# Projections of 64-row matmuls issued in two passes, and a layer-norm buffer pair reused as a fifth slot for down weights

## The chip, the cores and the metric

The kernel runs on one core of one Trainium2 chip. Its time is the device time in microseconds (us) of one launch, the median of three runs. A profile comes from one further execution, recorded by the hardware profiler.

## What is computed

Two layers, each an attention part A and a gated linear unit B, both added to their input. There are S = 2048 tokens, D = 576 features, H = 32 heads of 18, and F = 4608 hidden units. Both layers use the same weights.

```
x = x + A(layernorm(x));  x = x + B(layernorm(x))     # and the same again

A:  q, k, v = x @ wqkv, by heads
    phi(z)  = [softmax(z @ w_phi), softmax(-(z @ w_phi))]
    kv = sum_s phi(k)^T v;   z = sum_s phi(k)
    o  = phi(q) kv / (phi(q) z + 1e-6);   result o @ wo
B:  ((x @ w_gate) * (x @ w_up)) @ w_down
```

## The kernel before, in words

**Tiles.** Tokens come in 16 tiles of 128 and 8 blocks of 256. The gate and up weights stay in SBUF; the down weights do not fit and are streamed from HBM again for every block: 18 chunks of 288 KB per block and layer (`t_wd`, L1138), into a ring `wdr` of four slots. A slot is loaded again when the down matmuls of its chunk have read it.

**A planner sets the order.** Nothing in the kernel is issued by hand. Every piece of work is a generator (a thread) that yields requests: operations for an engine, a buffer from a pool, an event. `Sched.run` (L323) walks through all threads with a modelled clock per engine, picks the request with the lowest estimated start (minus a bias by priority, L430), and writes it to that engine's list. These lists, with the semaphore waits that the recorded reads and writes need, are the program. The planner's durations are constants in the code. So an edit of a priority or of an estimate changes the order on every engine.

**A block of B.** `t_bmain` (L1183) takes a lock on the PSUM banks and issues nine quads of 72 gate/up matmuls (`gu_quad`, L1149; matmuls on L1170). They are 64-row matmuls: 576 is four and a half times 128, and so the array runs as two halves of 64 rows side by side, one half for partitions 0 to 63 and one for 64 to 127. A quad is issued as four parts of 20, 20, 16 and 16 matmuls. In the first two parts each half writes banks of its own; in the last two it adds to the banks of the other half, and the first matmul there waits for the other half's last write (the `order` keys). Six of the eight PSUM banks serve the quads; once the quads hold all six, the lock is "open" (L1204), and threads that ask with a fourth argument of True may take the other two. ScalarE copies the gate result out (L1219), VectorE multiplies it with the up result into `hT` (L1221). Then `t_down` (L1228) runs 36 steps of two 512-column matmuls (L1243) and two 64-column ones (L1246) in full 128-row mode, and `t_bepi` adds the result to x.

**Projections.** Q, K, V and the output projection of a tile are made by `proj` (L864). It offers two forms and the planner takes the one that fits the mode TensorE is in: ten full matmuls (L870), or 18 row matmuls (L878) in which each half first makes five matmuls for a bank of its own and then four for the other's:

```
for i, h in enumerate((u, 1 - u)):
    for k in ((0, 1, 2, 3, 4) if i == 0 else (0, 1, 2, 3)):
...
            order=[("row", banks[h], 1 - u)] if i == 1 and k == 0 else []))
...
row = [o for pr in zip(half(0), half(1)) for o in pr]
return ("pe2", full, row)
```

All 18 are one request, so they stand together in TensorE's list. The first matmul of the second pass (number 11 of 18) waits for the first pass by a semaphore that TensorE itself raises; the planner's model prices that wait at `SEM_LAT`, 64 ns.

**What surrounds it.** `t_aout` makes phi(q) with `softmax_front` (L887), multiplies by kv (L1082), projects with wo and adds to x (L1130). `t_ain` makes phi(k), `t_v` makes v, `t_kv` (L1006) sums kv for layer 2. While block b of layer 1 runs its gate/up stage, the output projections and Q of the next block, and then K and V of the finished block for layer 2, go between its quads. Tiles from number 4 on project Q and the output only "in row", that is while a lock is open or the block is held up (`in_row`, L619). `softmax_front` needs one of two `psb` buffers and one of four `sm` buffers. The block after next waits for this kv sum (L1396).

**Layer norms.** `t_ln` (L805) takes one of two pairs of `xln` buffers, computes statistics on VectorE (L816, L821), three small ScalarE operations, the normalized tile on GpSimd or VectorE (L838), and transposes it by DMA on SP's queue (L856) or, with `fast`, on TensorE (L850).

**Queues.** All DMAs here are issued by SP, in the planner's order: down-weight loads (L1145), transposes of `xln` (L856), of phi(q) (eT, L1061) and of the attention output (oT, L1119), and the stores.

Of the kernel before, what the change touches and what calls it, by code (L numbers as in the profile page):

```python
# [14 lines left out]
SEM_LAT = 64.0  # L15


class Tracker:
# [45 lines left out]
    def ready_time(self, deps):  # L64
        t = 0.0
        for d in deps:
            f = self.fin.get(d, 0.0) + SEM_LAT
            if f > t:
                t = f
        return t  # L70
# [159 lines left out]
class _Thread:  # L230
    __slots__ = ("gen", "prio", "req", "name", "deps_cache", "est", "t_ready", "seq", "alt")
    _n = 0

    def __init__(self, gen, prio, name):
# [8 lines left out]
        self.t_ready = 0.0  # L243


class Sched:

    def __init__(self, tracker):
# [15 lines left out]
        self.open = False  # L264
        self.alt_cost = {"dve": 1.0, "pool": 1.0, "act": 1.0}
# [57 lines left out]
    def run(self):  # L323
        tr = self.tr
        while True:
            progressed = False
            again = True
            while again:
                again = False
                for th in list(self.threads):  # L330
                    while th.req is not None and th.req[0] not in ("ops", "alt", "pe2", "dma", "acq", "acqn"):
# [38 lines left out]
                        elif kind == "prio":  # L370
                            th.prio = r[1]
                            self._advance(th, None)
                        elif kind == "delay":
# [22 lines left out]
            for th in self.threads:  # L396
# [13 lines left out]
                elif r[0] == "pe2":  # L410
# [4 lines left out]
                    est = max(self.free_at["pe"], tr.ready_time(deps), th.t_ready)  # L415
                    th.alt = ("ops", "pe", ops)
                elif r[0] == "ops":
# [4 lines left out]
                    est = max(self.free_at[eng], tr.ready_time(deps), th.t_ready)  # L422
# [7 lines left out]
                key = (est - self.bias.get(int(th.prio), 0.0), -th.prio)  # L430
# [8 lines left out]
            if r[0] == "ops":  # L439
# [4 lines left out]
                for o in r[2]:  # L444
                    deps = tr.deps_for(eng, o.reads, o.writes, o.excl, True, o.order)
                    if not first:
                        t = max(t, tr.ready_time(deps))
# [24 lines left out]
            self._advance(th, None)  # L472
# [54 lines left out]
class K:  # L527
    def __init__(self, nc, A_x, A_wqkv, A_w_phi, A_wo, B_w_gate, B_w_up, B_w_down, out):
# [10 lines left out]
        self.urgent = 4  # L539
        self.prio0 = (4, 4)  # L540
# [9 lines left out]
    def alloc(self):  # L550
# [28 lines left out]
        self.xln = A("xln", [128, 2 * self.NXP, 640], BF16)  # L579
        self.st = A("st", [128, 2 * self.NXP, 12], F32)  # L580
# [31 lines left out]
        self.g_wd = [g("wd%d" % i) for i in range(self.NWD)]  # L612
# [192 lines left out]
    def t_ln(self, tiles, sig, fast=False):  # L805
        s = self
        x_sb, xln, st, mv, lnv, rstd, xT = s.x_sb, s.xln, s.st, s.mv, s.lnv, s.rstd, s.xT
        pair = yield ("acq", "xlnp")
        n = len(tiles)
        js = range(n)  # L810
        sl = [2 * pair, 2 * pair + 1]
# [8 lines left out]
        for j in js:  # L820
# [10 lines left out]
               reads=mvk + [("epst",)], writes=[("lnv", pair)]),  # L831
            Op(160, (lambda e: e.mul(nm[:, s0:s1], mean2, -1.0)),
               reads=mvk, writes=[("nmean", pair)]),
            Op(205, (lambda e: e.activation(rstd[:, s0:s1], lnv[:, s0:s1], ACTF.Exp, scale=-0.5)),  # L834
               reads=[("lnv", pair)], writes=[("rstd", pair)]),
        ])
        for j in js:
# [3 lines left out]
                reads=[("x", ss[j], 0), ("x", ss[j], 1), ("nmean", pair), ("rstd", pair)], writes=[("xln", sl[j])])])  # L841
                for eng, dur in (("pool", 800), ("dve", 340))[:1 + fast]])
        yield ("ops", "act", [Op(240, (lambda e: e.copy(xln[:, s0:s1, 576:640], xln[:, s0:s1, 512:576])),
                                 reads=[("xln", sl[j]) for j in js], writes=[("xlnt", pair)])])
# [208 lines left out]
    def t_aout(self, L, st_):  # L1053
# [80 lines left out]
        yield ("sig", ("x1", L, st_))  # L1134

    def t_wd(self, L):  # L1138
        s = self
        wdv = s.wd.rearrange("(f p) d -> p f d", p=128)  # L1140
# [323 lines left out]
```

## Time and profile before

| what | us |
|---|---|
| three runs | 1220.47, 1219.82, 1218.64 |
| median | 1219.82 |
| the profiled execution | 1216.11 |
| its span, first to last instruction | 1214.4 |
| mean granted TensorE clock in it | 0.978 of full |
| gate/up matmuls L1170, busy | 584.9 + 583.3 + 160.9 |
| down matmuls L1243 and L1246, busy | 292.7 and 222.0 |
| row projections L878, busy | 40.3 + 34.6 + 20.2 + 20.2 |

Busy times of matmuls that run side by side or overlap in the pipeline are each counted in full, so they sum to more than the span. A group's row gives the line, the engine, output<-inputs, the shape and the count, then busy time and the mean ns of one, then the idle time just before such instructions and what ended it. "PEld" is TensorE's weight load, "SPq" the DMA queue of SP. In the timeline each row is start, duration, engine, line, and in brackets the idle time before it with its releaser.

### The profile page before, as it was taken

How to read it: one execution, taken by the hardware profiler on the slowest of the kernel's cores; microseconds unless marked ns; L12 is line 12 of the kernel's file. 1: busy time of each engine (PE TensorE's matmuls, PEld its weight loads, DVE VectorE, ACT ScalarE, POOL GpSimd, SP SyncE). 2: the span in 40 equal slices, each digit the busy share in tenths (PEclk: the TensorE clock that was granted, in tenths of full speed). 3: DMA queues.
4: the chain of work that ended last, by engine and by line, in shares of the span. 5: the costliest groups of instructions: out<-in, count | busy, mean ns of one | idle time of the engine just before them, and what ended most of it. 6: DMA issues, size and time to landing. Idle time of an engine off the chain costs nothing.

```text
span 1214.4 us, 33952 instructions
## 1 busy us (share of the span) xinstructions
PE 1106.5 (91%) x15384; PEld 814.9 (67%) x15446; DVE 612.0 (50%) x1243; ACT 379.8 (31%) x917; POOL 264.6 (22%) x258
## 2 busy tenths in 40 slices
PE   5885999999999999999998589999999999999997
PEld 3663767768586776758585367685858585858584
DVE  7797554736464563635254566262526262524131
ACT  6774232514142341514042343040404040312120
POOL 5693121313122140412022222020202020200000
PEclk8897999999999999999999799999999999999999
DMA  7473145361614535170605111727272736363514
GB/s 174 113 290 92 32 112 118 53 178 33 187 34 132 88 80 140 33 193 19 176 13 149 47 26 42 193 33 197 32 197 23 185 44 173 49 155 72 156 32 147
DMA packets 183276, 128.84 MB, mean 106 GB/s; under 512 B 101595, under 2 KB 181979, under 8 KB 181979
## 3 DMA queue, kind: packets, MB, share of 16 engines
q1 hardware_dynamic: 183130, 126.66, 42.8%
q8 instruction: 121, 1.98, 0.7%
q14 instruction: 25, 0.20, 0.0%
HBM read 100.73 MB, written 2.36 MB: 85 GB/s over the span
## 4 chain that ended last, share of the span: by engine, by line
PE 71%; DMA 15%; DVE 7%; ACT 3%; POOL 1%; issue 1%; SPq 0%; DVEq 0%; POOLq 0%
PE ps L1170 45%; DMA wdr<-in_B_w_down_dram 15%; PE ps L1243 11%; PE ps L878 9%; DVE ss L935 2%; PE ps L870 2%; PE ps L1246 2%; PE ps L1082 1%; PE ps L982 1%; POOL dd L949 1%; DVE dd L920 1%; DVE mxmn L906 1%; DVE mxmn L901 1%; DVE hT L1221 1%; ACT dd L928 1%
## 5 line engine op out<-in xcount | busy, mean ns | idle before, releaser
L1170 PE MATMUL ps<-xT,Wg 64*128 64x256 bf16 x4608 | 584.9, 270 | 1.6 <-ACT xT L852 1.6
L1170 PE MATMUL ps<-xT,Wu 64*128 64x256 bf16 x4608 | 583.3, 270 | 1.5 <-DVE hT L1221 1.5
L1170 PEld LDWEIGHTS ps<-xT,Wg 64*128 64x128 bf16 x4608 | 432.2, 94 | 36.1 <-issue 3.3
L1170 PEld LDWEIGHTS ps<-xT,Wu 64*128 64x128 bf16 x4608 | 432.6, 94 | 29.8 <-DVE hT L1221 2.9
L1219 ACT CAST gsb<-ps 128x512 bf16<-128x512 f32 x288 | 167.7, 582 | 638.0 <-PE ps L1170 636.3
L1221 DVE TENSOR_TENSOR hT<-ps,gsb 128x512 bf16<-128x512 f32 x288 | 198.0, 690 | 262.8 <-ACT gsb L1219 262.7
L1243 PE MATMUL ps<-wdr,hT 128*128 128x512 bf16 x1090 | 292.7, 381 | 31.1 <-DMA wdr<-in_B_w_down_dram 29.4
L1243 PEld LDWEIGHTS ps<-wdr,hT 128*128 128x128 bf16 x1152 | 112.4, 98 | 183.1 <-DMA wdr<-in_B_w_down_dram 65.3
L1246 PE MATMUL ps<-wdr,hT 128*128 128x64 bf16 x1152 | 222.0, 193 | 4.6 <-DMA wdr<-in_B_w_down_dram 1.0
L949 POOL TENSOR_TENSOR dd<-dd,ss 128x576 bf16<-128x576 bf16 x124 | 142.7, 1172 | 210.8 <-ACT ss L943 210.7
L838 POOL TENSOR_SCALAR xln<-x_sb,nmean,rstd 128x576 bf16<-128x576 bf16 x58 | 47.0, 820 | 551.0 <-ACT rstd L834 551.0
L1170 PE MATMUL ps<-xT,Wr 64*128 64x256 bf16 x1152 | 160.9, 271 | 0.0
L1268 DVE TENSOR_TENSOR x_sb<-ps,x_sb 128x512 bf16<-128x512 f32 x32 | 21.9, 686 | 232.7 <-PE ps L1246 232.7
L1246 PEld LDWEIGHTS ps<-wdr,hT 128*128 128x128 bf16 x1152 | 113.0, 98 | 0.0
L935 DVE TENSOR_REDUCE ss<-dd 128x64 f32<-128x1152 bf16 x64 | 86.1, 1347 | 25.2 <-ACT dd L930 25.1
L911 POOL TENSOR_TENSOR dd<-psb,mxmn 128x576 bf16<-128x576 bf16 x62 | 72.0, 1163 | 86.4 <-DVE mxmn L901 86.4
L1170 PEld LDWEIGHTS ps<-xT,Wr 64*128 64x128 bf16 x1152 | 59.1, 95 | 7.2
L901 DVE TENSOR_REDUCE mxmn<-psb 128x32 f32<-128x576 bf16 x64 | 47.8, 746 | 23.5 <-ACT psb L898 22.9
L898 ACT CAST psb<-ps 128x288 bf16<-128x288 f32 x128 | 46.6, 400 | 30.1 <-PE ps L878 16.1
L928 ACT ACTIVATE dd<-dd 128x576 bf16<-128x576 bf16 x64 | 43.8, 684 | 38.3 <-DVE dd L920 38.1
L906 DVE TENSOR_REDUCE mxmn<-ps 128x16 f32<-128x288 f32 x128 | 51.9, 447 | 0.1
L920 DVE TENSOR_TENSOR dd<-ps,mxmn 128x288 bf16<-128x288 f32 x128 | 51.6, 445 | 0.0
(78 smaller groups left out, 777.1 us busy)
## 6 DMA issues: line engine op xcount, KB each, us to landing
wdr<-in_B_w_down_dram SPq DMA_DIRECT2D x288, 288.0 KB, 3.4
Wg<-in_B_w_gate_dram SPq DMA_DIRECT2D x4, 1152.0 KB, 13.1
Wu<-in_B_w_up_dram SPq DMA_DIRECT2D x4, 1152.0 KB, 15.3
x_sb<-in_A_x_dram SPq DMA_DIRECT2D x8, 288.0 KB, 3.3
out_dram<-x_sb SPq DMA_DIRECT2D x8, 288.0 KB, 3.6
Wraw<-in_A_wqkv_dram SPq DMA_DIRECT2D x8, 144.0 KB, 3.1
xT<-xln SPq DMA_TRANSPOSE x58, 2.7
Wv<-in_A_wqkv_dram SPq DMA_DIRECT2D x1, 576.0 KB, 4.3
```

What stands on the lines that cost most here:

```text
L878: out.append(Op(61, (lambda e, h=h, k=k, st=(i == 0 and k == 0), sp=(i == 1 and k == 3): e.matmul(s.ps[:, banks[h], 0:N], L[r, k, :], Wm[r ...
L901: ops = [Op(665, (lambda e: e.tensor_reduce(mxmn[:, pz, 0, :], p3, AX.X, ALU.max)), reads=[("psb", pz, 0), ("psb", pz, 1)], writes=[("mx", ...
L906: ops.append(Op(370, (lambda e, h=h, pv=pv: e.tensor_reduce(mxmn[:, pz, 1, 16 * h:16 * h + 16], pv, AX.X, ALU.min)), reads=[("pbd", bank)] ...
L911: yield ("alt", [(eng, [Op(dur, (lambda e: e.tensor_tensor(d1, p3, mxb, ALU.subtract)), reads=[("psb", pz, 0), ("psb", pz, 1), ("mx", pz)] ...
L920: ops.append(Op(370, (lambda e, d2h=d2h, pv=pv, mnbh=mnbh: e.tensor_tensor(d2h, pv, mnbh, ALU.subtract)), reads=[("pbd", bank), ("mn", pz, ...
L935: Op(1320, (lambda e: e.tensor_reduce(ss[:, sm, :].rearrange("p (b g) -> p b g", b=2), e4, AX.X, ALU.add)), reads=s.ddk(sm, 0) + s.ddk(sm, ...
L949: yield ("alt", [(eng, [Op(dur, (lambda e, ev=ev, rb=rb: e.tensor_tensor(ev, ev, rb, ALU.mult)), reads=s.ddk(sm, br) + [("ss", sm)], write ...
L1170: out.append(Op(54.3, (lambda e, bank=bank, cs=cs, lhsT=lhsT, rhs=rhs, st=st, sp=sp: e.matmul(ps[:, bank, cs], lhsT, rhs, start=st, stop=s ...
L1219: yield ("ops", "act", [Op(540, (lambda e, g=g, gb=gb: e.copy(gsb[:, g, :], ps[:, gb, :])), reads=[("gu", gb)], writes=[("gsb", g)], excl= ...
L1221: yield ("ops", "dve", [Op(625, (lambda e, g=g, ub=ub, p=p: e.tensor_tensor(hT[:, p, :], ps[:, ub, :], gsb[:, g, :], ALU.mult)), reads=[(" ...
L1243: ops.append(Op(d_pe(512), (lambda e, lhsT=lhsT, bank=bank, slot=slot, fi=fi, f=f: e.matmul(ps[:, bank, 0:512], lhsT, s.wdr[:, slot, fi, 0 ...
L1246: ops.append(Op(d_pe(64) + 3, (lambda e, lhsT=lhsT, sl=sl, slot=slot, fi=fi, f=f: e.matmul(ps[:, Z, 64 * sl:64 * sl + 64], lhsT, s.wdr[:, ...
```

## The change

A row projection becomes two requests, passes of 10 and 8 matmuls. Between them other threads' requests may be placed. For a wait of TensorE on itself the planner now assumes 450 ns (`PE_SELF`). While a lock is open, a projection's thread has a `boost`: its key is lowered by 500, or, if its estimated start is more than 100 ns past the time TensorE is free, raised by 1500. K and V of layer 2 for tiles 0 to 13 now also project only "in row".

After the last norm of the first attention, `t_grow` takes the second `xln` pair out of its pool, and `wdx`, a view of its bytes, joins the ring of down weights as slot 4. The dependencies of the norms are kept by slot instead of by pair, and the two single-tile norms at a layer's start or end share one pair.

The diff's core (repeated renamings of keys and passing of arguments left out):

```diff
+PE_SELF = 450.0
...
-    def ready_time(self, deps):
+    def ready_time(self, deps, eng=None):
...
         for d in deps:
-            f = self.fin.get(d, 0.0) + SEM_LAT
+            f = self.fin.get(d, 0.0) + (PE_SELF if eng == "pe" and d[0] == "pe" else SEM_LAT)
...
+                        elif kind == "boost":
+                            th.boost = r[1]
+                            self._advance(th, None)
...
-                    est = max(self.free_at["pe"], tr.ready_time(deps), th.t_ready)
-                    th.alt = ("ops", "pe", ops)
+                    est = max(self.free_at["pe"], tr.ready_time(deps, "pe"), th.t_ready)
+                    th.alt = ("ops", "pe", ops, self.pe_mode)
...
-                key = (est - self.bias.get(int(th.prio), 0.0), -th.prio)
+                late = th.boost and est > self.free_at["pe"] + 100.0
+                key = (est - self.bias.get(int(th.prio), 0.0) - (self.hold if late else th.boost), -th.prio)
...
-            self._advance(th, None)
+            self._advance(th, r[3] if th.req[0] == "pe2" else None)
...
+        self.wdx = AT("wdx", [128, CH, D], BF16, nc.lookup_mloc(self.xln).addr + 2560)
...
-    def t_ln(self, tiles, sig, fast=False):
+    def t_ln(self, tiles, sig, fast=False, slot=None):
...
-        pair = yield ("acq", "xlnp")
+        if slot is None:
+            pair = yield ("acq", "xlnp")
+            sl = [2 * pair, 2 * pair + 1]
+        else:
+            sl = [slot]
         n = len(tiles)
         js = range(n)
-        sl = [2 * pair, 2 * pair + 1]
+        key = lambda name: [(name, sl[j]) for j in js]
...
-               reads=mvk + [("epst",)], writes=[("lnv", pair)]),
+               reads=mvk + [("epst",)], writes=key("lnv")),
...
-                       [("xln", sl[j]), ("xlnt", pair)], [("xT", ss[j])], 128 * 640 * 2, False, True, 1250.0)
-        yield ("rel", "xlnp", pair)
+                       [("xln", sl[j]), ("xlnt", sl[j])], [("xT", ss[j])], 128 * 640 * 2, False, True, 1250.0)
+        if slot is None:
+            yield ("rel", "xlnp", pair)
...
         row = [o for pr in zip(half(0), half(1)) for o in pr]
-        return ("pe2", full, row)
+        if s.sc.open:
+            yield ("boost", s.rboost)
+        if (yield ("pe2", full, row[0:10])):
+            yield ("ops", "pe", row[10:])
+        yield ("boost", 0.0)
...
         s.vx_of[(L, st_)] = vxs
+        if L == 2 and st_ < NS - 2:
+            yield ("when", s.in_row)
         gots = yield ("acqn", ["pb"], 2, True)
         banks = [g_[1] for g_ in gots]
-        yield s.proj(st_, s.Wv, "Wv", banks)
+        yield from s.proj(st_, s.Wv, "Wv", banks)
...
-        sm = yield from s.softmax_front(st_, ps_, s.Wk, "Wk", 2 if st_ >= NS - 2 else 1 if L == 1 else 0)
+        sm = yield from s.softmax_front(st_, ps_, s.Wk, "Wk", 2 if st_ >= NS - 2 else 1 if L == 1 else 0, None, L == 2 and st_ < NS - 2)
...
+
+
+    def t_grow(self):
+        s = self
+        yield ("wait", ("xT", 1, NB - 1))
+        pool = s.sc.pools["xlnp"]
+        yield ("when", lambda: 1 in pool["free"])
+        pool["free"].remove(1)
+        yield ("rel", "wd", s.NWD, 0.0)
+
+    def wslot(self, slot):
+        return self.wdr[:, slot, :, :] if slot < self.NWD else self.wdx[:]
...
                 slot = yield ("acq", "wd")
                 s.wd_slot[(L, b, c)] = slot
-                yield ("dma", s.g_wd[slot], (lambda e, slot=slot, c=c: e.dma_start(s.wdr[:, slot, :, :], wdv[:, CH * c:CH * c + CH, :])),
-                       (), [("wdr", slot)], 128 * CH * D * 2, False, True)
+                yield ("dma", s.g_wd[slot], (lambda e, slot=slot, c=c: e.dma_start(s.wslot(slot), wdv[:, CH * c:CH * c + CH, :])),
+                       (), [("wdr", slot)] + ([("xln", 2), ("xln", 3), ("xlnt", 2), ("xlnt", 3)] if slot == s.NWD else []), 128 * CH * D * 2, False, True)
                 yield ("sig", ("wd", L, b, c))
...
                 ops.append(Op(d_pe(512), (lambda e, lhsT=lhsT, bank=bank, slot=slot, fi=fi, f=f: e.matmul(
-                    ps[:, bank, 0:512], lhsT, s.wdr[:, slot, fi, 0:512], start=(f == 0), stop=(f == NF - 1))),
...
         def pair_done(b):
             yield ("wait", ("x1", L, 2 * b))
             if b == 0:
-                yield ("go", s.t_ln([0], [("xTB1", L)], True), 11, "lnB%d_0a" % L)
+                pair = yield ("acq", "xlnp")
+                yield ("go", s.t_ln([0], [("xTB1", L)], True, 2 * pair), 11, "lnB%d_0a" % L)
                 yield ("wait", ("x1", L, 1))
-                yield ("go", s.t_ln([1], [("xTB2", L)], True), 11, "lnB%d_0b" % L)
+                yield ("go", s.t_ln([1], [("xTB2", L)], True, 2 * pair + 1), 11, "lnB%d_0b" % L)
                 yield ("wait", ("xTB1", L))
                 yield ("wait", ("xTB2", L))
+                yield ("rel", "xlnp", pair)
                 yield ("sig", ("xTB", L, 0))
                 return
...
         def k2():
             yield ("wait", ("x2t", L, 2 * b))
             if last:
+                pair = yield ("acq", "xlnp")
                 for j in range(2):
                     yield ("wait", ("x2t", L, 2 * b + j))
-                    yield ("go", s.t_ln([2 * b + j], [("xTk", j)], True), 11, "k2ln%d" % j)
+                    yield ("go", s.t_ln([2 * b + j], [("xTk", j)], True, 2 * pair + j), 11, "k2ln%d" % j)
                 for j in range(2):
                     yield ("wait", ("xTk", j))
+                    if j == 1:
+                        yield ("rel", "xlnp", pair)
                     yield ("go", s.t_ain(2, 2 * b + j), 11 + (2 - j) / 100.0, "ain2_%d" % (2 * b + j))
...
+        sc.launch(self.t_grow(), 9, "grow")
```

## The prediction, made before the changed kernel was run

> **What bounds the kernel now.** I read the page first (engines, then the chain that ended last), then the groups of instructions by line, the sources of the two suspect lines, and last the timeline of single blocks.
>
> ```profile
> span 1214.4 us, 33952 instructions
> PE 1106.5 (91%) x15384; PEld 814.9 (67%) x15446; DVE 612.0 (50%) x1243; ACT 379.8 (31%) x917; POOL 264.6 (22%) x258
> PE 71%; DMA 15%; DVE 7%; ACT 3%; POOL 1%; issue 1%; SPq 0%; DVEq 0%; POOLq 0%
> PE ps L1170 45%; DMA wdr<-in_B_w_down_dram 15%; PE ps L1243 11%; PE ps L878 9%; DVE ss L935 2%; PE ps L870 2%; PE ps L1246 2%; PE ps L1082 1%; PE ps L982 1%; POOL dd L949 1%; DVE dd L920 1%; DVE mxmn L906 1%; DVE mxmn L901 1%; DVE hT L1221 1%; ACT dd L928 1%
> ```
>
> TensorE is the bound, and beside it stand the down-weight loads (15% of the chain) and the 64-row projections (L878, 9%). From about 123 us the program is 16 GLU blocks: a gate/up stage of 648 matmuls (L1170), then a down stage of 72 matmul pairs (L1243 with 512 columns, L1246 with 64). The first 123 us and the layer change at 670 to 710 us are chains of other engines, which this change hardly touches.
>
> One projection between two gate/up quads, as the weight loads show it:
>
> ```profile
> 152.55 0.57 PEld L878 LDWEIGHTS ps<-Wq,xT 64*128 64x128 bf16 x10
> 153.52 0.36 PEld L878 LDWEIGHTS ps<-Wq,xT 64*128 64x128 bf16 x8 [0.40 <-PE ps L878]
> 153.91 0.09 PEld L1170 LDWEIGHTS ps<-xT,Wg 64*128 64x128 bf16 x1
> ```
>
> and who waited at that line in the whole run:
>
> ```profile
> its engine sat idle before it (us, times) until:
>   PE ps L878: 31.8, 80
> ```
>
> After ten loads TensorE stops 0.40 us for its own first pass: the second pass adds into the bank that the other 64 rows wrote. 80 times is every row projection there is (1440 matmuls of L878 / 18). Next the last down stage, which holds nothing but down matmuls: SP's issues, then the windows view (the middle of the stage, the whole stage, one gate/up stage of layer 1):
>
> ```profile
> 1190.02 14.81 SPq L1145 DMA_DIRECT2D wdr<-in_B_w_down_dram  x14
> core 0: us, PE busy (x) PEld busy (x) DVE busy (x) ACT busy (x) POOL busy (x), PEclk, DMA share, GB/s
> 1191.10:1207.10 16.00, 14.12 (x107) 6.61 (x108) 0.00 (x0) 0.00 (x0) 0.00 (x0) 1.00 0.87 256
> 1188.80:1209.60 20.80, 18.73 (x142) 8.98 (x144) 1.29 (x2) 0.58 (x1) 0.00 (x0) 1.00 0.68 199
> 190.50:237.30 46.80, 46.07 (x802) 38.12 (x801) 30.12 (x58) 20.19 (x49) 13.54 (x14) 1.00 0.37 51
> ```
>
> Four of the 18 chunks of a block are there when it starts, 14 are fetched inside it, each issued only when a slot is read out. The DMA engines are at 0.87, not at 1, while TensorE waits for them.
>
> **Change 1: the split projection.** Quads follow one another every 3.93 us without a projection (7.86 for two) and 5.30 with one (148.73 to 154.03), so a projection takes 1.37. Streaming, it would take 9 pairs: a gate/up pair of 256 columns comes every 0.109, so one of 288 every 0.1226, and nine 1.10. The stop therefore costs 0.27, not 0.40, since matmuls still run during part of it. All of it is on TensorE inside a saturated stage: 80 x 0.265 = 21.2 us. After the change the second pass is held back until its planned wait is over, and a gate/up part of 16 to 20 matmuls (0.87 to 1.09 us) goes between. That exceeds the 0.40 wait. Quads already do this: their third part waits on the first, 20 matmuls back, and the trace shows no gap (150.80 to 150.91). The waiting instruction would hold everything behind it on TensorE, but at most for the old 0.40. Passes and gate/up matmuls are all in 64-row mode, so no mode change is added; only a second pass that slips behind the end of the stage would add two, at 0.22 each (188.61 to 188.83 is one). I count nine in ten hidden: **-19 us** (bounds 0 and -21.2).
>
> **Change 2: the fifth slot.** A down pair comes every 0.245 us, so a stage needs 72 x 0.245 = 17.64, or 0.98 per chunk. What each stage takes beyond that and beyond the other matmuls in it (0.6 to 3.2 us) I took from the first and last weight load of each: 4.1, 2.4, 2.9, 2.1, 3.2, 3.5, 3.2, 4.4 in layer 1 and 3.4, 2.6, 3.1, 3.4, 3.1, 2.8, 2.5, 3.1 in layer 2, together 49.8 us. The waits view names 29.4 of it as TensorE waiting for the loads; the rest is refilling after each stop.
>
> How much does one more slot return? In the last stage the fifth chunk was used 4.1 after the start, and from then the interval is 294,912 B / 256 GB/s = 1.15 (1.11 by SP's issues: 14.44 / 13). Chunk 18 is then ready at 4.1 + 13 x 1.15 = 19.1 and needed at 17 x 0.98 = 16.7: 2.4 late, plus 0.7 of refilling, which is the 3.1 measured. With five slots one chunk more is there at the start: 4.1 + 12 x 1.15 = 17.9, late by 1.2, if the interval stays. But one more load is then in flight too. At a DMA share of 1 instead of 0.87 the interval would be 1.00, the last chunk ready at 16.1, nothing late. Halfway, at 1.07, it is 0.3 late. I take 0.6 per stage with refilling: 49.8 - 16 x 0.6 = **-40 us** (bounds: one interval per stage, 16 x 1.2 = -19, and -50).
>
> Here a rule weighs in. The Trainium skill (DMA: Bandwidth & Descriptors, Anatomy of one DMA), in its fit for the GpSimd path, makes a transfer a fixed 2.0 us plus its bytes at 436 GB/s: an estimate of 2.7 us for 288 KB, nearly all latency. By it a loop over five slots needs (0.98 + 2.7) / 5 = 0.74 per chunk, and every stop would vanish: -50. The page of this run has a median of 3.4 us to landing, on SP's queue, with the engines at 0.87, so loads queue behind each other. The row decides: -40, not -50.
>
> **Change 3: what pays for it.** The second layer-norm pair goes after the first layer's norms. Two norms per block remain: stats at 191.81 with transposes issued at 196.90, then stats at 206.15. With 2.5 us of issuing and 2.7 to landing a pair is held some 10 us, and the two begin 14 apart, so they don't meet; if they did, the later one waits up to 10 us, covered by the 47 us until the next block (259.57). Cost 0. At the start a fifth load joins four on SP (73.84, 13.17 us for all): 3.3 us more, then SP is idle until the eT transposes at 104.11. Cost 0 to 1. At a stage's end five loads instead of four stand ahead of the two oT transposes, about 1 us on data that is used 8 us after the stage ends (198.27, against 190.27). Cost 0. The other waits that the second pair's reuse adds are on transposes that landed long before.
>
> **Change 4: boost, and layer-2 K and V only inside gate/up stages.** Counts stay: K and V of tiles 0 to 13 are row projections already (252 / 18 = 14 each). They bunch earlier, where VectorE is busier, and each holds its two banks one part longer. The Trainium skill speaks against such a step (TensorEngine Tiling (Array Packing), PSUM Bottleneck): tiling speeds TensorE, not the emptying of PSUM, which can become the bound. If it did, the 19 us would not be seen. The row says 30.1 of 46.8 us busy on VectorE and 20.2 on ScalarE; in a stage 2.1 shorter that is 67% and 45%. Between 208 and 232 us VectorE is at 17.1 of 24. Only bunching can hurt: 0 to 1 us in seven stages, I take **+3 us**. The layer change may be planned differently, by 4 us either way; I take 0.
>
> **Sum.** -19 - 40 + 3 = -56. The profiled execution took 1216.1 (its span is 1214.4); the median of the runs stands 3.7 above that. So 1160 profiled and 1219.8 - 56 = 1164 as median.
>
> **Rivals.**
> - *The loads are at their limit* (0.14). The interval stays at 1.15 and the fifth slot gives only its head start. For: 0.87 of share, 1.00 at best against 0.98 needed. Against: the closed loop of issue after reading. Then 1219.8 - 19 - 19 + 3 = 1185.
> - *The projection's stop moves instead of going* (0.12): no gate/up part is ready between the passes, or gate/up waits for VectorE. For: two banks serve all projections. Against: L1170 waited 3.1 us for anyone in the whole run (1.6 at Wg, 1.5 at Wu, in the groups). Then 1219.8 - 40 = 1180.
> - *Slower: the second K tile misses its window* (0.08). Today it starts at 233.99, just after the stage's last gate/up matmul (233.97), and its key-value matmuls end at 247.68. Under the new condition a K that isn't admitted before the stage ends waits until the next block stands still for it, since that block waits for this key-value sum: 13.7 us open in each of the stages 2 to 7, 82 in all, so 1164 + 82 = 1246; from five of six stages on the kernel is slower. It decides by the softmax buffer that K needs: the second Q gives it back at about 223, 11 us before the stage ends. Today one projection per quad is let in, which is what puts K so late; with the boost it goes at the next part. So I hold it unlikely.
>
> **How the numbers follow.** Main case 0.62, 1148 to 1178 (all 71 us returned gives 1149, the lower parts of both gains about 1178). Mixtures near no change 0.04, split evenly over the three signs. Within 0.2% (2.4 us) counts as no change, about what a measurement of this kernel can tell. Faster 0.89, same 0.02, slower 0.09. The range 1148 to 1190 takes in the first two rivals and leaves out the slow one.
>
> **What would show it.** Right: the line of the projections has no 0.40 stop in most of the 80, its 18 matmuls appear as 10 and 8 with gate/up between; gate/up stages with eight projections shrink from 46.2 to about 44; down stages from 20.7 to about 18.2 in the last block; the chain's share of down loads falls from 15% to a few per cent; DMA share in a down stage rises above 0.87. Wrong: SP's issues still 1.11 apart (first rival), L1170 waiting for VectorE (second), or gaps of over 10 us ahead of blocks 2 to 7 (third).

## The result, and the profile after

The changed kernel takes **1177.51 us** (median of four runs, 1173.66 to 1178.24); the kernel before took 1220.14 beside it (1218.64 to 1221.16). The ratio is 0.9645, 95% interval 0.9621 to 0.9669: 42.6 us less. The forecast was 1164, which is 56 us less. The profiled execution took 1178.24, its span is 1176.5 (1214.4 before), its mean granted TensorE clock 0.978, as before.

The page first: span, engines, and the two rows of the chain that ended last (gate/up is now L1203, down L1276 and L1279, the row projection L892, the full one L884).

```profile
span 1176.5 us, 34009 instructions
PE 1088.5 (93%) x15446; PEld 840.3 (71%) x15446; DVE 605.8 (51%) x1243; ACT 378.1 (32%) x917; POOL 264.5 (22%) x258
PE 74%; DMA 11%; DVE 8%; ACT 4%; POOL 1%; issue 1%; SPq 0%; DVEq 0%; POOLq 0%
PE ps L1203 41%; PE ps L1276 16%; PE ps L892 9%; DMA wdr<-in_B_w_down_dram 5%; DMA oT<-dd 4%; PE ps L884 2%; PE ps L1279 2%; DVE ss L953 2%; DMA wdx<-in_B_w_down_dram 1%; PE ps L1102 1%; PE ps L1002 1%; DVE mxmn L924 1%; DVE mxmn L919 1%; POOL dd L967 1%; DVE dd L938 1%; DVE hT L1254 1%
```

The down loads fell from 15% of the chain to 6 (5 for the ring of four, 1 for the fifth slot). But there is an entry that was not there before: `oT<-dd`, the transposes of the attention output, 4%. It makes up with them the 11% that DMA still holds.

The waits view of TensorE says the same (waited for: us in total, times, longest). Before:

```profile
PE ps L1243 <- DMA wdr<-in_B_w_down_dram: 29.4, 52, 1.6
```

and after:

```profile
PE ps L1276 <- DMA wdr<-in_B_w_down_dram: 11.3, 15, 1.8
...
PE ps L892 <- DMA oT<-dd: 7.8, 8, 1.6
...
PE ps L1276 <- DMA wdx<-in_B_w_down_dram: 1.6, 3, 1.1
```

29.4 us in 52 waits for down loads became 12.9 in 18, the fifth slot's included. And the source view of the row projections, where before stood one line, "PE ps L878: 31.8, 80":

```profile
its engine sat idle before it (us, times) until:
  DMA oT<-dd: 17.8, 16
  DVE x_sb L1150: 2.5, 14
...
```

TensorE's stop for itself is gone, in all 80 projections. A new wait is in its place, for data that was never waited for before. The view adds TensorE's two rows, matmuls and weight loads, so the 17.8 is not a time lost; the matmuls' own part is the 7.8 above.

The last down stage has no attention in it, in the forecast's trace and in this one. SP's issues:

```profile
1154.58 3.31 SPq L1178 DMA_DIRECT2D wdr<-in_B_w_down_dram  x4
1158.49 0.37 SPq L1178 DMA_DIRECT2D wdx<-in_B_w_down_dram  x1
1159.47 3.49 SPq L1178 DMA_DIRECT2D wdr<-in_B_w_down_dram  x4
1163.57 0.37 SPq L1178 DMA_DIRECT2D wdx<-in_B_w_down_dram  x1
1164.55 2.90 SPq L1178 DMA_DIRECT2D wdr<-in_B_w_down_dram  x3
```

and the windows view of its middle, of the same stretch of the stage before it, and of one gate/up stage of layer 1:

```profile
core 0: us, PE busy (x) PEld busy (x) DVE busy (x) ACT busy (x) POOL busy (x), PEclk, DMA share, GB/s
1155.50:1170.00 14.50, 14.14 (x115) 7.02 (x112) 0.00 (x0) 0.00 (x0) 0.00 (x0) 1.00 0.89 266
...
187.30:233.50 46.20, 45.05 (x794) 39.80 (x792) 30.93 (x61) 21.09 (x51) 14.66 (x14) 1.00 0.30 58
1102.00:1116.00 14.00, 13.99 (x115) 7.09 (x114) 0.00 (x0) 0.00 (x0) 0.00 (x0) 1.00 0.94 282
```

13 chunks are fetched inside the stage, not 14. They are (1164.55 + 2.90 - 0.37 - 1154.58) / 12 = 1.04 apart, where it was 1.11; in the stage before, the engines carry 0.94 and TensorE is busy 13.99 of 14.00. The last stage takes 18.22 (20.72 before; the forecast said about 18.2), the one before it 17.70 (20.15).

**Where the 37.9 us of span came from.** From the weight loads of each trace I cut the run into gate/up stages (first gate/up load to first down load), down stages (to the last down load), and the layer change. The sums of the 16 stages, in us, for all kernels that this text needs:

| kernel | first stage starts | gate/up stages | down stages | layer change | span |
|---|---|---|---|---|---|
| before | 123.00 | 693.2 | 350.7 | 39.36 | 1214.4 |
| after | 125.49 | 685.8 | 318.1 | 39.01 | 1176.5 |
| the split alone | 123.55 | 683.1 | 347.6 | 39.37 | 1201.7 |
| the fifth slot alone | 125.22 | 693.4 | 314.3 | 38.93 | 1180.0 |
| oT planned 3.2 us later | 125.74 | 684.8 | 312.4 | 40.48 | 1171.6 |
| oT planned 5.5 us later | 126.06 | 674.0 | 312.0 | 39.81 | 1160.0 |
| the same, 64 small matmuls ahead | 123.46 | 675.1 | 313.3 | 38.54 | 1158.6 |

Down stages gave 32.6 us (forecast 40), gate/up stages 7.4 (forecast 19 - 3 = 16), and 2.5 were lost ahead of the first stage. The large miss is in the gate/up stages: they lost their 80 stops and came out hardly shorter. A stage with eight projections took 47.0 us before in this cut and takes 45.5 to 46.7 now; the forecast had written 46.2 and 44.

**The new wait.** One gate/up stage of layer 2, starting at 811.54. SP's queue around its start, then the chain in the first microseconds:

```profile
807.73 3.31 SPq L1178 DMA_DIRECT2D wdr<-in_B_w_down_dram  x4
811.08 2.54 SPq L1139 DMA_TRANSPOSE oT<-dd  x2
```

```profile
811.08 6.16 DMA oT<-dd
817.24 0.05 issue
817.29 0.78 PE ps L892 x9
```

and the weight loads of the two projections that follow:

```profile
817.28 0.48 PEld L892 LDWEIGHTS ps<-Wo,oT 64*128 64x128 bf16 x10 [1.92 <-DMA oT<-dd]
...
818.90 0.45 PEld L892 LDWEIGHTS ps<-Wo,oT 64*128 64x128 bf16 x8
...
820.48 0.09 PEld L892 LDWEIGHTS ps<-Wo,oT 64*128 64x128 bf16 x1
820.73 0.48 PEld L892 LDWEIGHTS ps<-Wo,oT 64*128 64x128 bf16 x9 [0.16 <-DVE x_sb L1150]
```

The passes are 10 and 8, with gate/up matmuls between them (817.76 to 818.90): the split works as forecast. But the first output projection of the stage stands behind one quad of 72 matmuls, 3.9 us after the start, and its input lands 5.7 after it. Everything behind it in TensorE's list waits too. In the whole run eight gate/up stages have such a stop of the matmuls, two in layer 1 and six in layer 2.

### The profile page after: what moved, and what is told of

It reads as the page before. It is cut to its first block, busy times and chain, and to the rows that moved or that the text cites. A ratio compares the mean times of both kernels' runs of the same rounds, so it can differ in the third digit from the quotient of the medians.

```text
span 1176.5 us, 34009 instructions
## 1 busy us (share of the span) xinstructions
PE 1088.5 (93%) x15446; PEld 840.3 (71%) x15446; DVE 605.8 (51%) x1243; ACT 378.1 (32%) x917; POOL 264.5 (22%) x258
## 3 DMA queue, kind: packets, MB, share of 16 engines
q8 instruction: 121, 1.98, 0.7%
## 4 chain that ended last, share of the span: by engine, by line
PE 74%; DMA 11%; DVE 8%; ACT 4%; POOL 1%; issue 1%; SPq 0%; DVEq 0%; POOLq 0%
PE ps L1203 41%; PE ps L1276 16%; PE ps L892 9%; DMA wdr<-in_B_w_down_dram 5%; DMA oT<-dd 4%; PE ps L884 2%; PE ps L1279 2%; DVE ss L953 2%; DMA wdx<-in_B_w_down_dram 1%; PE ps L1102 1%; PE ps L1002 1%; DVE mxmn L924 1%; DVE mxmn L919 1%; POOL dd L967 1%; DVE dd L938 1%; DVE hT L1254 1%
## 5 line engine op out<-in xcount | busy, mean ns | idle before, releaser
L1203 PE MATMUL ps<-xT,Wu 64*128 64x256 bf16 x4608 | 589.7, 270 | 2.3 <-DVE hT L1254 1.9
L1203 PE MATMUL ps<-xT,Wg 64*128 64x256 bf16 x4608 | 585.1, 270 | 1.6 <-ACT xT L865 1.6
L1203 PEld LDWEIGHTS ps<-xT,Wu 64*128 64x128 bf16 x4608 | 432.1, 94 | 23.3 <-DVE hT L1254 5.3
L1203 PEld LDWEIGHTS ps<-xT,Wg 64*128 64x128 bf16 x4608 | 425.8, 94 | 28.8 <-issue 3.3
L1276 PE MATMUL ps<-wdr,hT 128*128 128x512 bf16 x924 | 241.8, 380 | 11.5 <-DMA wdr<-in_B_w_down_dram 11.3
L1203 PE MATMUL ps<-xT,Wr 64*128 64x256 bf16 x1152 | 202.4, 271 | 0.0
L1279 PE MATMUL ps<-wdr,hT 128*128 128x64 bf16 x924 | 178.1, 193 | 0.0
L1276 PEld LDWEIGHTS ps<-wdr,hT 128*128 128x128 bf16 x924 | 90.3, 98 | 121.3 <-DMA wdr<-in_B_w_down_dram 18.6
L1203 PEld LDWEIGHTS ps<-xT,Wr 64*128 64x128 bf16 x1152 | 92.1, 95 | 5.0
L1279 PEld LDWEIGHTS ps<-wdr,hT 128*128 128x128 bf16 x924 | 90.5, 98 | 0.0
L1276 PE MATMUL ps<-wdx,hT 128*128 128x512 bf16 x228 | 64.3, 380 | 1.9 <-DMA wdx<-in_B_w_down_dram 1.6
## 6 DMA issues: line engine op xcount, KB each, us to landing
Wg<-in_B_w_gate_dram SPq DMA_DIRECT2D x4, 1152.0 KB, 13.2
```

The costliest lines, as they stand in the source:

```text
L1203: out.append(Op(54.3, (lambda e, bank=bank, cs=cs, lhsT=lhsT, rhs=rhs, st=st, sp=sp: e.matmul(ps[:, bank, cs], lhsT, rhs, start=st, stop=s ...
L1276: ops.append(Op(d_pe(512), (lambda e, lhsT=lhsT, bank=bank, slot=slot, fi=fi, f=f: e.matmul(ps[:, bank, 0:512], lhsT, s.wslot(slot)[:, fi, ...
L1279: ops.append(Op(d_pe(64) + 3, (lambda e, lhsT=lhsT, sl=sl, slot=slot, fi=fi, f=f: e.matmul(ps[:, Z, 64 * sl:64 * sl + 64], lhsT, s.wslot(s ...
```

## The experiments

Ratios are against the kernel before on the same chip, with the 95% interval.

**1. The split alone** and **2. the fifth slot alone.** The first never launches the thread that hands over the second layer-norm pair; the second makes the projection one request again and takes out the boost, the planner's 450 ns and the condition on K and V (V's place is shown, K's is of the same kind):

```diff
-        sc.launch(self.t_grow(), 9, "grow")
```

```diff
-PE_SELF = 450.0
+PE_SELF = SEM_LAT
...
-        if s.sc.open:
-            yield ("boost", s.rboost)
-        if (yield ("pe2", full, row[0:10])):
-            yield ("ops", "pe", row[10:])
-        yield ("boost", 0.0)
+        yield ("pe2", full, row)
...
-        if L == 2 and st_ < NS - 2:
-            yield ("when", s.in_row)
...
```

> The changed kernel without its fifth slot: the second layer-norm pair stays in its pool, down weights keep four slots. First theory (the split's saving is mostly given back because the boost places the output projection before its transposed input has landed): down stages as before (20 to 23 us), gate/up stages as in the changed kernel, so only some 8 us are gained: 1212, between 1206 and 1216. Rival (the split saves its 19 us, and the two parts get in each other's way only together, a stage that ends sooner leaving less time for the transposes): 1201 or less.

> The changed kernel with its fifth slot, but each row projection again one request of 18 matmuls, no boost, no 450 ns in the plan, K and V of layer 2 not bound to the gate/up stages. Both theories give the fifth slot what the down stages lost between the two profiles, 33 us: 1187. If the parts help each other (a shorter gate/up stage matters to the loads) it is above 1192; if they hinder each other, below 1182.

Measured: split alone 1206.80, ratio 0.9918 (0.9892 to 0.9943), so 10.0 us; slot alone 1181.04, ratio 0.9708 (0.9676 to 0.9741), so 35.7 us. Their sum is 45.7, the whole change 42.6: within their intervals, some 3 to 4 us each, they add up, and no hindrance between the two is seen. The slot's part is near its 40. The split's part is half of its 19, and it is so without the slot: its gate/up stages sum to 683.1, 10.1 less than before. The split alone has the waits of the ring nearly as before, 25.6 us in 54 times; the slot alone 10.1 in 17. In the split alone the wait for the oT transposes is there as well, with four loads ahead instead of five, but smaller: 2.8 us on the matmuls, where the changed kernel has 7.8.

**3. The oT data planned later, by 3.2 us**, and **6. by 5.5 us**, from the time that the planner has SP's issue end (3200.0 in one, 5500.0 in the other; nothing waits on the chip, the planner only believes the data to come later and so orders the projection later):

```diff
+            if st_ >= s.urgent:
+                yield ("delay", s.sc.free_at["sp"] + 5500.0)
```

> The changed kernel, but the planner is told that the transposed input of an output projection (tiles from 4 on) is there 3.2 us after SP's issue ends. Nothing else differs on purpose. First theory: the waits of projection matmuls on the oT transposes (7.8 us on matmuls, 17.8 us on weight loads) go, and the gate/up stages of layer 2 shrink from 41.5 to 42.2 us to about 40.6: 1167 to 1171. Rival (the gate/up stages are long because of PSUM and VectorE, and the projection merely waits where it would wait anyway): no change, 1176 to 1179.

> The changed kernel, the planner told that the transposed input of an output projection is there 5.5 us after SP's issue ends, instead of 3.2 in the earlier try, which moved no projection past the landing (15.0 us of weight loads still waited for oT, against 17.8). Theory (the output projection is placed ahead of its data): the wait on oT goes to below 3 us and layer-2 gate/up stages come to about 40.6, in all 8 to 10 us: 1166 to 1170. Rival (the stages are long for another reason): the wait goes and the time stays at 1175 to 1178.

The smaller delay gave 1175.52, ratio 0.9665 (0.963 to 0.97), an expectation missed: it moved no projection past its landing, the weight loads still idle 15.0 us in 16 waits for oT, and the gate/up stages sum to 684.8. The larger one gave **1162.69** (1161.73 to 1164.11), ratio 0.957 (0.9551 to 0.9589), below the 1166 to 1170 expected. Its source view of the row projections has no line for oT any more:

```profile
its engine sat idle before it (us, times) until:
  DVE dd L938: 1.7, 10
  DVE x_sb L1152: 0.9, 3
  DMA xT<-xln: 0.2, 1
```

and the stage that answers to the one above starts at 804.23 with its first projection 6.9 us later, not 5.7:

```profile
811.12 0.57 PEld L892 LDWEIGHTS ps<-Wo,oT 64*128 64x128 bf16 x10
812.61 0.45 PEld L892 LDWEIGHTS ps<-Wo,oT 64*128 64x128 bf16 x8
```

No bracket: it waits for nothing. The transposes were issued at 803.76, as early as before relative to the stage. The gate/up stages sum to 674.0, so 11.8 less than in the changed kernel and 19.2 less than before, which is the forecast's -19. A layer-2 stage with four projections takes 41.04 (42.11 before, 41.53 to 42.98 in the changed kernel). This placement is what the split's gain had gone into: TensorE's stops on oT are 7.8 of the 11.8; the rest was not taken apart. The down stages are 6.1 us shorter as well, but that can't be put down to the placement: the smaller delay, which moved no projection past its data, has 312.4 there too, and TensorE's waits for down loads range from 7.5 to 14.2 us over kernels with the same ring (experiments 3 and 7).

**4. Without the boost**, and **5. without the boost and without K/V's condition** (taken out as in 2):

```diff
-        self.rboost = 500.0
+        self.rboost = 0.0
```

> The changed kernel with the boost at 0 (which also takes away the hold): passes still split, still priced at 450 ns, K and V still bound to the gate/up stages. First theory: projections go where they went before the change, so nothing waits for oT, and the split alone saves most of its 21 us: 1164 to 1170. Rival (without the boost K misses its window, or second passes follow the first without anything between): above 1180.

> The changed kernel with the boost at 0 and K and V of layer 2 no longer bound to the gate/up stages; passes stay split, the fifth slot stays. The run without boost alone left two gaps of 27 us ahead of blocks, where K had missed its stage, while its layer-2 gate/up stages were the shortest of all (39.18). If the missed K is all that was wrong there, this one keeps the 39.18 and has no gaps: about 1168, between 1162 and 1174. If the boost itself is needed (for the order on VectorE or for the banks), gaps remain and it is above 1180.

Without the boost: 1214.85, ratio 0.9984 (0.9963 to 1.0005): the whole gain is gone. TensorE's first waits are now

```profile
PE ps L1102 <- DMA eT<-dd: 42.5, 5, 14.2
PE ps L1276 <- DMA wdr<-in_B_w_down_dram: 11.6, 21, 2.0
```

and there are 27.83 and 27.28 us between a down stage and the next gate/up stage ahead of blocks 2 and 5, and 51.83 at the layer change. Each pass now takes a place of its own between two whole quads, as the chain shows (start, duration, what):

```profile
280.90 4.04 PE ps L1203 x72
284.94 0.61 PE ps L892 x10
285.55 3.93 PE ps L1203 x72
289.48 0.49 PE ps L892 x8
289.97 3.93 PE ps L1203 x72
```

With one pass per quad, eight projections need 16 places and a stage has nine. The second K and V come too late for the stage, their condition then lets them in only when a block is held up, and block 2 stands still until their kv sum is made: the slower rival of the forecast, in two of its six places (two more have 4.35 and 2.84 us) and at twice its 13.7 us, because the boost that it was said to depend on is gone. Output and Q projections run in the gap too, and the 13.8 us that TensorE waits there are for eT, which stands ahead of the kv sum in its list. The two passes together take 0.61 + 0.49 = 1.10, the forecast's streaming time.

With K/V's condition gone too: 1177.32, ratio 0.969 (0.9672 to 0.9707), the time of the changed kernel, and not the 1162 to 1174 expected. No gap is left between blocks, and no wait for oT, but the second K and V now run as full projections behind the gate/up matmuls. Gate/up and down stages together come to 650.9 + 341.2 = 992.1, 6.1 more than with oT planned later, and the layer change takes 49.91, 10.1 more: 16.2, and the spans are 15.9 apart (1175.9 and 1160.0). Why the layer change is longer I did not follow. So the boost is no luxury of the split: it keeps two passes inside one quad, and K and V inside the stage.

**7. The fifth slot handed over later**, at the end of the first block's attention instead of after the last norm, to see whether the slot costs the 2.5 us at the start:

```diff
-        yield ("wait", ("xT", 1, NB - 1))
+        yield ("wait", ("xTB", 1, 0))
```

> The changed kernel, the fifth slot joining the ring only when the norms of the first block of the first gated unit are done, not right after the attention's norms. If the first gate/up stage starts 2.5 us later than before the change because the planner sees a fifth load ahead of the eT transposes and reorders VectorE, it starts at about 123.3 again and the time falls by 2: 1175. If the late start has another cause it stays at 125.5 and 1177.

Measured 1177.80, ratio 0.9692 (0.9671 to 0.9713): no gain. The first stage starts at 123.90, but then takes 45.55 where it took 43.08; what was early was given back. The trace shows why: that stage now holds 36 of the matmuls that multiply phi(q) by kv (L1102), where the changed kernel's holds 24. The slot does reorder the start: it brings one eT transpose, and with it these 12 matmuls, ahead of the stage. The split alone, which has no slot, has 36 and 45.58. Counted to the end of the first gate/up stage, before stands at 167.3, the changed kernel at 168.6, the split alone at 169.1 and this one at 169.5; kernels with the slot and an unchanged order there reach from 166.5 to 169.1 (64 small matmuls ahead, oT 5.5 us later). So the 2.5 us at the start are in part work that changed places, and of the rest one profile of each kernel can't tell.

**8 to 10. What is left in the down stages.** 72 pairs of 0.245 make 17.64. In the changed kernel the last but one stage is at 17.70, others up to 21.38 (23.69 ahead of the layer change). The DMA table of the changed kernel's page has other queues than the data's (packets, MB, share of the 16 engines):

```profile
q1 hardware_dynamic: 183130, 126.66, 41.9%
q8 instruction: 121, 1.98, 0.7%
q14 instruction: 24, 0.20, 0.1%
```

On q8 there are 121 packets of 16 KB each, one for every 256 of TensorE's 30,892 matmuls and weight loads (30,892 / 121 = 255), and one lasts 0.88 to 1.86 us. The theory is that the DMA engine which carries it brings its part of a chunk later. In the changed kernel's trace (the stage ahead of the layer change left out, where attention runs) all seven stops of 0.5 us or more on a down load end 2.2 to 3.5 us after the start of such a packet. The last but one stage, whose packets come 0.6 us before its start and 17.3 us after it, has no stop. That is only a coincidence in time, so I moved the packets.

The first attempt added one-element memsets on engines that have nothing to do in the last two down stages, to have more instructions fetched (the spare tile and the later oT data are not shown):

```diff
+        if L == 2 and b >= NB - 2:
+            for eng, n, one in (("pool", 480, s.fill[0:1, 0:1]), ("dve", 220, s.fill[0:1, 1:2])):
+                yield ("ops", eng, [Op(60, (lambda e, one=one: e.memset(one, 1.0)), reads=[("hT", NP - 1)], writes=[("fill", eng)])
+                                    for _ in range(n)])
```

> This is the version with the later oT data (1162.69 us), and in each of the last two down stages GpSimd runs 480 and VectorE 220 one-element memsets into a spare tile from the moment that the stage begins; both engines have nothing else to do there. The memsets add nothing to what the stage's matmuls need; what they add is instructions to be fetched, some 1,400 of them. So far 14 of the 16 down stages hold an instruction packet of 16 KB (0.88 to 1.95 us on one DMA engine), most of their stops come 2.2 to 3.9 us after one, and the last but one stage, at 1082.70 to 1100.55 in that version, holds no packet in any trace and took 17.70 to 18.00 us. Theory: a packet of instructions holds up one sixteenth of a down load and that stops the matmuls, so the last but one stage now holds one to three packets, shows a stop of 0.3 to 1.8 us some 2 to 4 us after a packet, and takes 18.3 to 20 us; the last stage the same; 1164 to 1167 in all. Rival: the stops come from the loop of five slots and the packets only happen to fall there; packets appear, the last but one stage stays at 17.7 to 18.1 with no stop above 0.3, and the time stays within 1161 to 1164.

It took 1210.68, ratio 0.9952 (0.9935 to 0.9969), and tells little. The edit itself has a fault: the memsets count as readers of `hT`, so VectorE's next write there waited for all of GpSimd's, and the last gate/up stage took 68.64 us for 35.48. And the 1,400 added instructions came on q14, 35 packets there instead of 24, of 8 KB each; q8 still had its 121. The last but one stage took 18.19, with one stop of 0.31. Undecided.

The second attempt shifts TensorE's own packets. 64, or 32, one-column matmuls go ahead of the first transposes, where TensorE waits 5.3 us for its first data. All other instructions keep their order on every engine; each packet comes 128, or 64, instructions earlier in the program. Both are made from the version with oT 5.5 us later:

```diff
+            if which == "k" and kt == 0:
+                yield ("ops", "pe", [Op(0, (lambda e, bank=bank: e.matmul(s.ps[:, bank, 0:1], s.ident[:], s.ident[:, 0:1], start=True, stop=True)),
+                                        reads=[("ident",)], writes=[("pbd", bank)], excl=[("pb", bank)]) for _ in range(64)])
```

> The version with the later oT data (1162.69 us), with 64 one-column matmuls put ahead of the first transposes, where TensorE waits 5.30 us for its first data; nothing else differs in any engine's order. In that version a 16 KB instruction packet comes once in 256 instructions of TensorE (213 to 303 between two in the trace). 64 matmuls are 128 instructions with their weight loads, so each packet comes 128 instructions earlier in the program: some 8 us earlier in a down stage (288 instructions in 18 us). Theory: the packet causes the stops of the down stages, so they move with it. The last but one stage, which had no packet and no stop on a load, gets one about half way and a stop of 0.3 to 1.5 us 2 to 4 us behind it; stages 9 to 13, which had one 4 to 8 us after their start and stops of 0.25 to 0.9 us, lose it to the stage before or to its first us, where five slots are full, and lose these stops. Time 1159 to 1165. Rival: the loop of five slots causes the stops; they stay in the stages and at the chunks where they were (0.35, 0.76, 0.25, 0.89 us in stages 10 to 13, none in the last but one).

> As the one before with 32 matmuls, 64 instructions, some 4 us earlier in a down stage. Theory: the last but one stage gets a packet about 12 us after its start and a stop of 0.3 to 1.5 us behind it; the packets of stages 9 to 13 come 1 to 4 us after the start and their stops are gone or below 0.4 us; the last stage's packet comes about 8 us after its start with its stop behind it. Time 1159 to 1165. Rival: the stops stay where they were.

Times 1162.97 (ratio 0.9542, 0.951 to 0.9574) and 1162.77 (0.9534, 0.9501 to 0.9567): as without the shift. But the stops moved. When the stop ends and how long TensorE had waited, in three stages of layer 2, with the packet's start:

| stage | no shift | 64 matmuls | 32 matmuls |
|---|---|---|---|
| 11 | packet +6.7 us, stop +9.5 of 0.76 | packet +15.5, stop +18.3 of 0.52 | packet +1.9, no stop above 0.45 |
| 13 | packet +7.9, stop +10.6 of 0.89 | packets +0.7 and +16.7, no stop above 0.30 | packet +3.3, no stop above 0.46 |
| 14 | packets -0.6 and +16.5, no stop | packet +8.6, none above 0.25 | packet +13.2, stop +15.3 of 1.23 |

(times from the stage's start; stages counted from 0). The expectations of 8 and 9 say that stage 14, the last but one, holds no packet; the trace has one at each of its edges and none between. Stage 14 had stopped for at most 0.31 in the changed kernel and in every one made from it with the boost, five slots and the packets in place; with the shift of 32 it got its packet at 1099.77, and this is the weight loads' timeline behind it (the bracket is the weight loads' idle time, 1.53; the matmuls' own is 1.23):

```profile
1100.27 0.10 PEld L1284 LDWEIGHTS ps<-wdr,hT 128*128 128x128 bf16 x1
1101.90 0.10 PEld L1281 LDWEIGHTS ps<-wdr,hT 128*128 128x128 bf16 x1 [1.53 <-DMA wdr<-in_B_w_down_dram]
```

In both shifted kernels together 10 of 14 stops of 0.5 us or more end 2.1 to 3.4 us after a packet's start, though a stretch of 1.9 to 4.1 us behind the packets covers only some 2.2 of a stage's 19 us. Where the packet falls matters: in the changed kernel and the two shifted ones together, such a stop follows none of 16 packets in the first 4 us of a stage, 6 of 15 from 4 to 10 us, and 11 of 16 later (the stage ahead of the layer change and packets in a stage's last 2 us left out). As the stops moved with the packets and nothing else in the order changed, I take the packets for the cause of most long stops; that full slots absorb the early ones is my reading, not tested. Not all stops are theirs: four of the 14, 0.51 to 0.63 us, have no packet at that distance, and stage 14 took its packet at +8.6 without one. Moving the packets only moved the loss; I know of no edit here that avoids it.

## Why the prediction was right and wrong

**Direction, and what bounds the kernel: right.** TensorE with two kinds of stop; both were cut, and the time fell.

**Change 1, the projection's stop, -19: right in mechanism, and returned in full only with another placement.** No self-wait is left in 80 projections. The changed kernel kept 7.4 us of stage time and the split alone 10.1; with oT planned later it is 19.2. (For the price of a mode change the forecast points to 188.61 to 188.83; the place is 1188.61 to 1188.83, and the 0.22 stands.)

**Change 3, "Cost 0" for the oT transposes: the step that failed.** It said that five loads instead of four stand ahead of them, "about 1 us on data that is used 8 us after the stage ends". The 8 us were read from the trace of before, where the projection stood behind two quads (198.27, against 190.27). They were not a property of the data but of the order, and the same change moves the order: with the boost the projection goes at the first part after one quad, 3.9 us after the start. In the stage shown the data takes 6.16 us from issue and lands 5.7 us after the start. Over all 28 transposes that SP issues from oT's line, the time from issue to landing was, before and after:

```profile
DMA to landing us min/median/max: 2.6/4.1/5.5
DMA to landing us min/median/max: 2.6/4.7/6.2
```

The fifth load made them 0.6 to 0.7 later, so the "about 1 us" was right. But the new placement leaves some 0.5 before the stage's start and 3.9 after it, 4.4 in all, less than even the median. The split alone, with four loads ahead (2.6/4.2/5.5), waits too: the earlier use makes the wait, and the later landing lengthens it, from 2.8 to 7.8 us on the matmuls. How the 11.8 divide between the two is not settled: the split alone stands 9.1 above the 674.0, but 2.5 of that are its first stage with its 12 more matmuls.

The price is 685.8 - 674.0 = 11.8 us of gate/up time in the profiles. By time it is less sharp: the ratios 0.9645 and 0.957 are 0.0075 apart, 9 us, while experiments 7 and 6, timed on one chip (1177.80 and 1162.69), are 15.1 apart, 7.1 of it in down stages by their profiles.

**Change 2, the fifth slot, -40: right, a little high.** 32.6 us of stage time in the changed kernel, 36.4 in the slot alone, 38.7 with oT later; by times 35.7. The forecast left 0.6 us per stage; the changed kernel's down stages stand 32.6 below, so 7.4 / 16 = 0.46 more than that is left. The interval was taken at 1.07, measured 1.04 in the last stage. Most of the long stops that are left, which the sum did not have, follow instruction packets (experiments 9 and 10). The price that the fit of the Trainium skill (DMA: Bandwidth & Descriptors, Anatomy of one DMA) would give, every stop gone at -50, was not reached; chunks landed in a median of 3.6 us in the last stage, longer than the 3.4 of before and than the 2.7 that the forecast worked out from the fit. With one more in flight they queue a little more, as the forecast chose.

**Change 3 at the start, "Cost 0 to 1": not settled.** The first stage starts 2.5 us later in this profile, 0.5 to 3.1 with the slot in others; to the end of that stage it is 1.3, and part of the start is work that changed places (experiment 7).

**Change 4, +3 for VectorE: not seen.** With the boost in force, oT later and all 80 stops gone, the gate/up stages are at the full -19.2; VectorE has 30.93 of 46.20 us in the stage shown. What the boost costs is the early oT. What it saves is the whole gain as long as K and V are bound to the stages (experiment 4); without it and without that condition the time is the changed kernel's (experiment 5).

**Rivals.** *Loads at their limit*: no, 0.94 of share in a stage without stops. *The projection's stop moves instead of going*: not by its own mechanism (gate/up parts were there, and VectorE was no limit), but by another that the list did not have; its time of 1180 was the nearest to the 1177.5, by luck. *K misses its window*: not in this kernel; real as soon as the boost alone is taken away.

**The sum.** Forecast -19 - 40 + 3 = -56. The version that delays oT in the plan has -19.2 - 38.7 in its stages, + 3.1 ahead of the first and + 0.4 at the layer change: -54.4 of span; its time, 1162.69, stands beside 1215.70 of the kernel before on its chip. The terms were sized rightly, the slot's a little high; the one that was set to nothing took some 12 us, between 9 and 15 by times. That 1177.51 still lies inside the forecast's main case, 1148 to 1178, half a microsecond from its end, is luck: that end stood for smaller gains of both parts, and not for a wait on oT.

## What to carry to other kernels

When an edit lets work go earlier, look up every input of that work in the trace: when it lands, not when it was used, and put the landing beside the new time of use. A slack read from the old order is worth nothing once the same edit changes the order. And a planner that orders by estimates must know the landing behind a full queue: here a delay of 5.5 us in its model, with no change on the chip but the order, gave back 11.8 us of gate/up time.

## What the runs showed of the hardware

TensorE's instructions show up among the DMA traffic: a 16 KB packet for 256 instructions, 121 in a run, 0.88 to 1.98 us each in the kernels that were timed here. When such a packet fell 4 us or more into a down stage, TensorE stopped for 0.5 to 1.8 us, some 2 to 3.5 us later, in 17 of 31 cases; within the first 4 us, in none of 16 (changed kernel and the two shifted ones, counted as in experiments 8 to 10). The 1,400 instructions added on GpSimd and VectorE came as 11 more packets of 8 KB on another queue.

A DMA transpose of oT landed later with a fifth down load ahead of it: 4.7 us in the median and 6.2 at most (4.6 and 6.1 with the slot alone), against 4.1 and 5.5 before (4.2 and 5.5 with the split alone); the least was 2.6 in all four.
